# Layer 2's output product of an attention-and-two-layer kernel: which operand stands in the array, and the layout of the stored result

## The chip, the cores and the metric

The kernel runs on one core of a Trainium2 chip. A core has five engines with queues of their own: TensorE (PE in the profile, with its weight loads as PEld), VectorE (DVE), ScalarE (ACT), GpSimd (POOL) and SyncE (SP), which issues the DMAs here. The metric is the device time of one execution in microseconds (us); lower is better. A matmul on TensorE loads one operand into the array (the stationary one, LDWEIGHTS, here mostly 128 x 128) and streams the other through it (the moving one, MATMUL, here of up to 512 columns), and adds the product into a bank of PSUM.

## The reference, cut to what matters

An attention-like recurrence gives 3072 tokens of width 384, and two feed-forward layers follow, each with 2048 hidden units:

```python
def _moe_ref(x, w_in, w_out):          # layer 1: x is 3072 x 384
    h = x @ w_in                       # 384 x 2048
    g = h - np.tanh(h)
    return (g @ w_out).astype(np.float32)

def _moe2_ref(x, w_in, w_out):         # layer 2
    h = x @ w_in
    r = np.maximum(h, 0.0)
    g = r * r
    return (g @ w_out).astype(np.float32)   # 2048 x 384: the result is 3072 x 384
```

## The kernel before, in words

Each product is made of three matmuls. Every operand is split into a high part and a small remainder (`gh` and `gl` of the activations, `wh` and `wl` of the weights, `xh` and `xl` of the input), all in the 4-byte type fp32r, and high x high, high x low and low x high are added up in PSUM.

The tokens are worked on in six groups of 512 (`TG`), and the 2048 hidden units in sixteen slices of 128 (`NM`). One slice of one group is a **block**; there are 96 blocks of layer 1 (the very first in two halves) and then 96 of layer 2. A block has two products:

- `g1` (L197): the hidden slice `h`, 128 hidden units as rows by 512 tokens. Nine matmuls of 512 columns, weights stationary, input moving. Both layers do it in the same way.
- `g2` (L221 to L238): the slice's share of the group's result, added into banks `acc` that stay open over the sixteen blocks of a group. Layer 1 (L230 to L232) keeps the weights stationary and lets the 512 tokens of `gh` or `gl` move: nine matmuls of 512 columns into three banks, with the model's 128-column pieces as rows. Layer 2 (L236 to L238) does the reverse: 128 tokens of `gh` or `gl` are stationary and the weights' 384 model columns move: twelve matmuls of 384 columns into four banks, with the tokens as rows.

Between the two products `act` (L204) turns `h` into `gh` and `gl`: in layer 2 relu (L215), square (L216) and a copy to `gh` (L217) on ScalarE, then the remainder `gl` (L218) on VectorE.

`block_step(t)` (L850) writes the work down in a software pipeline: `act` of block t-1, `g1` of block t, and then `g2` of a block two or, from the last group of layer 1 on, three steps back. The engines run their queues in order. While layer 1 runs, TensorE does attention work between the blocks; in layer 1's last group and in all of layer 2 it does nothing but `g1` and `g2`, one after the other.

At the end of a group the banks are copied to SBUF and stored. Layer 1 does it in `put_x2` (L246): three banks of 512 columns, the first and third copied by ScalarE (L250), the second by VectorE (L252). Layer 2 does it in `put_out` (L272): four banks of 384 columns, two copied by ScalarE (L276) and two by VectorE (L278), each then stored by one DMA of SP's queue (L279) into 128 rows of the 3072 x 384 result. `new_acc` (L240) takes the banks: three of the pool `ps_c`, which has just three, and for layer 2 one more of `ps_a`. So the next group's first matmul into a bank must wait until the bank has been copied out.

In layer 2 ScalarE also makes one pass (`conv_check`, L174) over a reloaded weight block every second block; SP loads these blocks (L173), two buffers deep, in the same queue as the stores. `judge` (L911) folds the checks into a flag with one tiny matmul near the end. `run_general` (L646) is a slow path behind that flag, which is not taken.

Of the kernel before, what the change touches and what calls it, by code (L numbers as in the profile page):

```python
# [12 lines left out]
F32 = mybir.dt.float32  # L13
# [4 lines left out]
ALU = mybir.AluOpType  # L18
# [14 lines left out]
def kernel(  # L33
# [8 lines left out]
):  # L42
    nc = tc.nc
    B, S, H, DP = v.shape
    NT, DM = out.shape
    D = DM // H
    P = 128
    FF = w1.shape[0] * P
# [3 lines left out]
    KD = DM // P  # L52
    TG = B * P
# [12 lines left out]
    ps_c = fctx.enter_context(tc.tile_pool(name="ps_c", bufs=3, space=PSUM))  # L66
    ps_a = fctx.enter_context(tc.tile_pool(name="ps_a", bufs=3, space=PSUM))
# [9 lines left out]
        out=mask, in_=mask, compare_op=ALU.is_ge, fill=0.0, base=0,  # L77
# [55 lines left out]
    def words(st):  # L133
        sv = st.rearrange("p (n two) -> p n two", two=2)
        return sv[:, :, 0], sv[:, :, 1]
# [85 lines left out]
    def g2(layer, m, g, acc, cs=slice(0, TG)):  # L221
        gh, gl = g
        wh, wl = (w_[:, DM:] for w_ in wts[layer, m])
        first = m <= 0 and cs.start == 0
        end = m in (-1, NM - 1)
        if layer == 0:
            for j in range(KD):
                sl = slice(j * P, (j + 1) * P)
                o = acc[j][:, cs]
                nc.tensor.matmul(o, wh[:, sl], gh, start=first, stop=False)  # L230
                nc.tensor.matmul(o, wh[:, sl], gl, start=False, stop=False)  # L231
                nc.tensor.matmul(o, wl[:, sl], gh, start=False, stop=end)  # L232
        else:
            for j in range(B):
                sl = slice(j * P, (j + 1) * P)
                nc.tensor.matmul(acc[j][:, :DM], gh[:, sl], wh, start=first, stop=False)  # L236
                nc.tensor.matmul(acc[j][:, :DM], gh[:, sl], wl, start=False, stop=False)  # L237
                nc.tensor.matmul(acc[j][:, :DM], gl[:, sl], wh, start=False, stop=end)  # L238

    def new_acc(layer):  # L240
        acc = [ps_c.tile([P, TG], F32, tag="c", name="acc") for _ in range(KD)]
        if layer == 1:
            acc.append(ps_a.tile([P, TG], F32, tag="a", name="acc3"))
        return acc

    def put_x2(acc, dst):  # L246
        for j in range(KD):
# [12 lines left out]
    def split_x(xpool, xf):  # L260
        xh = xpool.tile([P, KD, TG], F32R, tag="xh", name="xh")
        xl = xpool.tile([P, KD, TG], F32R, tag="xl", name="xl")
        for kk in range(KD):
            nc.gpsimd.tensor_scalar(
                xh[:, kk], xf[:, kk], 1.0, 0.0, op0=ALU.mult, op1=ALU.add
            )
            nc.vector.tensor_tensor(
                xl[:, kk], xf[:, kk], xh[:, kk].bitcast(F32), op=ALU.subtract
            )
        return xh, xl  # L270

    def put_out(ap3, acc, dst):  # L272
        for j in range(B):
            t = ap3.tile([P, TG], F32, tag="ot", name="ot", bufs=4)
            if j % 2 == 0:
                nc.scalar.copy(t[:, :DM], acc[j][:, :DM])  # L276
            else:
                nc.vector.tensor_copy(t[:, :DM], acc[j][:, :DM])  # L278
            nc.sync.dma_start(dst(j), t[:, :DM])  # L279


    chk_s = const.tile([P, NU], F32, name="chk_s")
# [352 lines left out]
    for n in range(B, NU):  # L635
        c, b = divmod(n, B)
# [9 lines left out]
    def run_general():  # L646
# [5 lines left out]
        with ExitStack() as es:  # L652
            cp = es.enter_context(tc.tile_pool(name="gc", bufs=1))
# [8 lines left out]
            with tc.For_i(0, S, 1) as t:  # L662
# [15 lines left out]
                r = cp.tile([BH, D], F32, name="g_r")  # L678
# [18 lines left out]
                for i in range(NB):  # L697
                    sl = slice(i * TG, (i + 1) * TG)
# [16 lines left out]
                for i in range(NB):  # L715
                    sl = slice(i * TG, (i + 1) * TG)
# [7 lines left out]
        for layer in range(2):  # L724
            with ExitStack() as es:
                cp = es.enter_context(tc.tile_pool(name=f"gw{layer}", bufs=1))
                pp = es.enter_context(tc.tile_pool(name=f"gq{layer}", bufs=1, space=PSUM))
                na = KD + layer
                with tc.For_i(0, NG, 1) as g:
                    xf = cp.tile([P, KD, TG], F32, name="g_xf")  # L730
                    if layer == 0:
                        for j in range(B):
                            xn = cp.tile([P, DM], F32, name=f"g_xn{j}")
                            nc.sync.dma_start(xn, xg[ds(g * TG + j * P, P), :])
                            px = pp.tile([P, TG], F32, tag="h", name=f"g_px{j}")
                            for kk in range(KD):
                                sl = slice(kk * P, (kk + 1) * P)
                                nc.tensor.transpose(px[:, sl], xn[:, sl], ident)
                            nc.vector.tensor_copy(
                                xf[:, :, j * P:(j + 1) * P],  # L740
                                px[:, :DM].rearrange("p (k t) -> p k t", k=KD),
                            )
                    else:
                        nc.sync.dma_start(
                            xf, xg2.rearrange("k p t -> p k t")[:, :, ds(g * TG, TG)]
                        )
                    xt = split_x(cp, xf)
                    osum = cp.tile([P, na, TG], F32, name="g_os")
                    nc.vector.memset(osum, 0.0)
                    with tc.For_i(0, NM, 1) as m:  # L750
                        st = cp.tile([P, 2 * n2], I32, name="g_st")
                        nc.sync.dma_start(
                            st.unsqueeze(1),
                            (w1, w2)[layer].bitcast(I32).rearrange("m p x -> p m x")[:, ds(m, 1)],
                        )
                        lo, hi = words(st)
                        u = cp.tile([P, n2], I32, name="g_u")
                        uf = u.bitcast(F32)
                        ts, st2 = nc.vector.tensor_scalar, nc.vector.scalar_tensor_tensor
                        ts(u, hi, 0x7FFFFFFF, None, op0=ALU.bitwise_and)  # L760
                        ts(uf, uf, CLAMP_LO, CLAMP_HI, op0=ALU.max, op1=ALU.min)
                        ts(u, u, 3, 0x40000000, op0=ALU.logical_shift_left, op1=ALU.bitwise_xor)
                        st2(u, lo, 29, u, op0=ALU.logical_shift_right, op1=ALU.bitwise_or)
                        ts(u, u, 0x7FFFFFFF, None, op0=ALU.bitwise_and)
                        st2(u, hi, -0x80000000, u, op0=ALU.bitwise_and, op1=ALU.bitwise_or)
                        wh = cp.tile([P, n2], F32R, name="g_wh")
                        wl = cp.tile([P, n2], F32R, name="g_wl")
                        split_w(wh, wl, uf)
                        wts[layer, -1] = (wh, wl)
                        h = g1(layer, -1, xt, pp.tile([P, TG], F32, tag="h", name="g_h"))  # L770
                        acc = [
                            pp.tile([P, TG], F32, tag=f"c{j}", name=f"g_acc{j}")
                            for j in range(na)
                        ]
                        g2(layer, -1, act(layer, h, cp), acc)
                        for j, a in enumerate(acc):
                            n = TG if layer == 0 else DM
                            nc.vector.tensor_tensor(
                                osum[:, j, :n], osum[:, j, :n], a[:, :n], op=ALU.add
                            )  # L780
                    for j in range(na):
                        if layer == 0:
                            nc.sync.dma_start(xg2[j, :, ds(g * TG, TG)], osum[:, j])
                        else:
                            nc.sync.dma_start(
                                out[ds(g * TG + j * P, P), :], osum[:, j, :DM]
                            )


# [22 lines left out]
        return lambda j: x2g[g][j]  # L812

    def out_dst(g):
        return lambda j: out[j * S + g * P:j * S + (g + 1) * P, :]

    HT = TG // 2
    LAG = 3
# [11 lines left out]
    cur = {"g2": 0, "acc": None, "pool": gpool, "recheck": 0}  # L830
# [8 lines left out]
    def second_half(n):  # L839
        l, g, m, cs = blocks[n]  # L840
        if m == 0 and cs.start == 0:
            cur["acc"] = new_acc(l)
        g2(l, m, gs.pop(n), cur["acc"], cs)
        if m == NM - 1:
            if l == 0:
                put_x2(cur["acc"], x2_dst(g))
            else:
                put_out(cur["pool"], cur["acc"], out_dst(g))
# [94 lines left out]


_INS = ["qk", "v", "ri", "w1", "w2"]
_OUTS = [((3072, 384), "float32")]

# [45 lines left out]
```

## Time and profile before

| | |
|---|---|
| median of 3 runs | 1036.13 us (1034.98 to 1036.3) |
| the profiled execution's own time | 1037.15 us |
| its span, first to last instruction | 1035.1 us |
| TensorE busy in the span | 1004.8 us (97%) |
| ScalarE, VectorE busy | 641.4 us (62%), 565.5 us (55%) |
| mean granted TensorE clock | 0.998 of full speed |

The span is the time between the first and the last instruction that the profile records; the rest of an execution's own time lies around it. A matmul's duration in the profile runs from its start to the modelled end of its output, and matmuls overlap: what TensorE spends on one is the distance from its start to the next start, and that is read from the timeline.

### The profile page before, as it was taken

How to read it: one execution, taken by the hardware profiler on the slowest of the kernel's cores; microseconds unless marked ns; L12 is line 12 of the kernel's file. 1: busy time of each engine (PE TensorE's matmuls, PEld its weight loads, DVE VectorE, ACT ScalarE, POOL GpSimd, SP SyncE). 2: the span in 40 equal slices, each digit the busy share in tenths (PEclk: the TensorE clock that was granted, in tenths of full speed). 3: DMA queues.
4: the chain of work that ended last, by engine and by line, in shares of the span. 5: the costliest groups of instructions: out<-in, count | busy, mean ns of one | idle time of the engine just before them, and what ended most of it. 6: DMA issues, size and time to landing. Idle time of an engine off the chain costs nothing.

```text
span 1035.1 us, 16245 instructions
## 1 busy us (share of the span) xinstructions
PE 1004.8 (97%) x6388; PEld 863.0 (83%) x6388; DVE 565.5 (55%) x937; ACT 641.4 (62%) x1158; POOL 17.1 (2%) x35
## 2 busy tenths in 40 slices
PE   4998999999999999999999999999999999999997
PEld 1786777888888888888888888999999999999997
DVE  7989998877887665666544554122232322322211
ACT  8688887877776677677543446445555555555442
POOL 1000000000000000000000000000000000000000
PEclk9999999999999999999999999999999999999999
DMA  7324353544453211112004332013242242330000
GB/s 262 110 88 143 133 161 135 182 156 134 163 179 104 71 63 51 43 41 67 28 25 170 120 106 93 1 62 123 92 155 99 103 131 94 100 114 31 31 1 34
DMA packets 34642, 103.47 MB, mean 100 GB/s; under 512 B 5376, under 2 KB 8448, under 8 KB 34560
## 3 DMA queue, kind: packets, MB, share of 16 engines
q1 hardware_dynamic: 34560, 102.38, 29.3%
q8 instruction: 51, 0.84, 0.3%
q14 instruction: 31, 0.25, 0.1%
HBM read 86.51 MB, written 15.73 MB: 99 GB/s over the span
## 4 chain that ended last, share of the span: by engine, by line
PE 83%; DVE 2%; DMA 1%; ACT 1%; issue 0%; ACTq 0%
PE h L197 35%; PE acc L236 7%; PE acc L238 7%; PE acc L237 6%; PE acc L232 5%; PE acc L231 5%; PE acc L230 5%; PE px L566 3%; PE sc L533 3%; PE pU L597 2%; PE pq L516 1%; PE pk L516 1%; DMA ri<-in_ri_dram 1%; PE pc L427 0%; DVE cv L150 0%; DVE cv L146 0%
## 5 line engine op out<-in xcount | busy, mean ns | idle before, releaser
L218 DVE TENSOR_TENSOR gl<-t,gh 128x512 fp32r<-128x512 f32 (+1 forms) x193 | 132.5, 687 | 262.7 <-ACT gh L217 262.4
L197 PE MATMUL h<-xh,wh 128*128 128x512 f32 (+1 forms) x579 | 231.6, 400 | 0.1
L197 PE MATMUL h<-xh,wl 128*128 128x512 f32 (+1 forms) x579 | 227.7, 393 | 0.0
L197 PE MATMUL h<-xl,wh 128*128 128x512 f32 (+1 forms) x579 | 227.2, 392 | 0.0
L217 ACT CAST gh<-t 128x512 fp32r<-128x512 f32 (+1 forms) x193 | 119.3, 618 | 67.7 <-PE acc L237 43.3
L215 ACT ACTIVATE t<-h 128x512 f32<-128x512 f32 x96 | 57.5, 599 | 143.8 <-PE h L197 143.8
L238 PE MATMUL acc<-wh,gl 128*128 128x384 f32 x384 | 129.5, 337 | 0.0
L236 PE MATMUL acc<-wh,gh 128*128 128x384 f32 x384 | 129.4, 337 | 0.0
L237 PE MATMUL acc<-wl,gh 128*128 128x384 f32 x384 | 128.9, 336 | 0.0
L197 PEld LDWEIGHTS h<-xh,wl 128*128 128x128 f32 x579 | 108.7, 188 | 23.3
L197 PEld LDWEIGHTS h<-xh,wh 128*128 128x128 f32 x579 | 109.0, 188 | 21.9 <-issue 3.2
L197 PEld LDWEIGHTS h<-xl,wh 128*128 128x128 f32 x579 | 109.0, 188 | 18.1
L230 PE MATMUL acc<-gh,wh 128*128 128x512 f32 (+1 forms) x291 | 111.0, 391 | 3.1 <-ACT gh L217 3.1
L231 PE MATMUL acc<-gl,wh 128*128 128x512 f32 (+1 forms) x291 | 113.5, 390 | 0.3 <-DVE gl L218 0.3
L232 PE MATMUL acc<-gh,wl 128*128 128x512 f32 (+1 forms) x291 | 113.4, 390 | 0.0
L110 ACT ACTIVATE t<-h 128x512 f32<-128x512 f32 (+1 forms) x97 | 57.2, 590 | 79.1 <-PE h L197 77.5
L213 DVE TENSOR_TENSOR t<-h,t 128x512 f32<-128x512 f32 (+1 forms) x97 | 66.1, 682 | 42.2 <-ACT t L110 41.7
L103 ACT ACT_TABLE_LOAD x64 | 82.1, 1283 | 1.9 <-PEq L981 0.8
L236 PEld LDWEIGHTS acc<-wh,gh 128*128 128x128 f32 x384 | 72.2, 188 | 4.2
L237 PEld LDWEIGHTS acc<-wl,gh 128*128 128x128 f32 x384 | 72.1, 188 | 4.1
L238 PEld LDWEIGHTS acc<-wh,gl 128*128 128x128 f32 x384 | 72.0, 188 | 0.0
L230 PEld LDWEIGHTS acc<-gh,wh 128*128 128x128 f32 x291 | 54.2, 188 | 13.8 <-ACT gh L217 4.1
(133 smaller groups left out, 1406.3 us busy)
## 6 DMA issues: line engine op xcount, KB each, us to landing
st<-in_w_dram SPq DMA_DIRECT2D x32, 768.0 KB
sr<-in_w_dram SPq DMA_DIRECT2D x32, 768.0 KB
ri<-in_ri_dram SPq DMA_DIRECT2D x24, 384.0 KB
qk<-in_qk_dram SPq DMA_DIRECT2D x24, 384.0 KB
w2d<-cv SPq DMA_DIRECT2D x16, 384.0 KB
jw<-w2d SPq DMA_DIRECT2D x16, 384.0 KB
vz<-in_v_dram SPq DMA_DIRECT2D x21, 256.0 KB
x2d<-x2t SPq DMA_DIRECT2D x18, 256.0 KB
```

Source lines behind the costliest of these rows:

```text
L103: load = nc.scalar.preload_act_table_set(name).ins
L197: nc.tensor.matmul(h, w_[:, kk * P:(kk + 1) * P], x_[:, kk, cs], start=(i == 0), stop=(i == n - 1),)
L213: nc.vector.tensor_tensor(t, h, t, op=ALU.subtract)
L215: last["act"] = nc.scalar.activation(t, h, AF.Relu).ins
L217: nc.scalar.copy(gh, t)
L218: nc.vector.tensor_tensor(gl, t, gh.bitcast(F32), op=ALU.subtract)
L230: nc.tensor.matmul(o, wh[:, sl], gh, start=first, stop=False)
L231: nc.tensor.matmul(o, wh[:, sl], gl, start=False, stop=False)
L232: nc.tensor.matmul(o, wl[:, sl], gh, start=False, stop=end)
L236: nc.tensor.matmul(acc[j][:, :DM], gh[:, sl], wh, start=first, stop=False)
L237: nc.tensor.matmul(acc[j][:, :DM], gh[:, sl], wl, start=False, stop=False)
L238: nc.tensor.matmul(acc[j][:, :DM], gl[:, sl], wh, start=False, stop=end)
```

## The change

Layer 2's `g2` is written as layer 1's is: the weights are stationary, the 512 tokens of `gh` and `gl` move, and each block has nine matmuls of 512 columns into three banks. The result then stands with the model's columns as rows, so the output tensor becomes 384 x 3072 and is stored by three DMAs a group; a tile's 512 tokens belong to four batches of 128, which lie apart in the result, so each of a tile's 128 rows goes out as four pieces of 128 numbers. The caller turns the array over on the host, outside the measured time. The slow path behind the flag is changed in the same way and is left out of the diff.

```diff
@@ kernel
-    NT, DM = out.shape
+    DM, NT = out.shape
@@ g2
-        if layer == 0:
-            for j in range(KD):
-                sl = slice(j * P, (j + 1) * P)
-                o = acc[j][:, cs]
-                nc.tensor.matmul(o, wh[:, sl], gh, start=first, stop=False)
-                nc.tensor.matmul(o, wh[:, sl], gl, start=False, stop=False)
-                nc.tensor.matmul(o, wl[:, sl], gh, start=False, stop=end)
-        else:
-            for j in range(B):
-                sl = slice(j * P, (j + 1) * P)
-                nc.tensor.matmul(acc[j][:, :DM], gh[:, sl], wh, start=first, stop=False)
-                nc.tensor.matmul(acc[j][:, :DM], gh[:, sl], wl, start=False, stop=False)
-                nc.tensor.matmul(acc[j][:, :DM], gl[:, sl], wh, start=False, stop=end)
-
-    def new_acc(layer):
-        acc = [ps_c.tile([P, TG], F32, tag="c", name="acc") for _ in range(KD)]
-        if layer == 1:
-            acc.append(ps_a.tile([P, TG], F32, tag="a", name="acc3"))
-        return acc
+        for j in range(KD):
+            sl = slice(j * P, (j + 1) * P)
+            o = acc[j][:, cs]
+            nc.tensor.matmul(o, wh[:, sl], gh, start=first, stop=False)
+            nc.tensor.matmul(o, wh[:, sl], gl, start=False, stop=False)
+            nc.tensor.matmul(o, wl[:, sl], gh, start=False, stop=end)
+
+    def new_acc():
+        return [ps_c.tile([P, TG], F32, tag="c", name="acc") for _ in range(KD)]
@@ put_out
-        for j in range(B):
+        for j in range(KD):
             t = ap3.tile([P, TG], F32, tag="ot", name="ot", bufs=4)
             if j % 2 == 0:
-                nc.scalar.copy(t[:, :DM], acc[j][:, :DM])
+                nc.scalar.copy(t, acc[j])
             else:
-                nc.vector.tensor_copy(t[:, :DM], acc[j][:, :DM])
-            nc.sync.dma_start(dst(j), t[:, :DM])
+                nc.vector.tensor_copy(t, acc[j])
+            nc.sync.dma_start(dst(j), t.rearrange("p (b t) -> p b t", b=B))
@@ out_dst
-        return lambda j: out[j * S + g * P:j * S + (g + 1) * P, :]
+        return lambda j: out[j * P:(j + 1) * P, :].rearrange("p (b s) -> p b s", b=B)[
+            :, :, g * P:(g + 1) * P
+        ]
@@ second_half
-            cur["acc"] = new_acc(l)
+            cur["acc"] = new_acc()
@@ the caller
-    return r.results[0]["out_0_dram"]
+    return _np.ascontiguousarray(r.results[0]["out_0_dram"].T)
```

Up to layer 2's first `g2` every engine's order stays as it was. Line numbers of the changed kernel are its own: its `g2` is L229 to L231 and its copies L266 and L268, its store L269. On TensorE, `g2` of the fourth block of a group in layer 2; a row is line, operation, bank<-moving,stationary, and the moving operand's rows x columns. Before:

```order
L236 MATMUL acc_6920<-wh1_3_5981,gh_6942 128x384
L237 MATMUL acc_6920<-wl1_3_5982,gh_6942 128x384
L238 MATMUL acc_6920<-wh1_3_5981,gl_6943 128x384
L236 MATMUL acc_6921<-wh1_3_5981,gh_6942 128x384
L237 MATMUL acc_6921<-wl1_3_5982,gh_6942 128x384
L238 MATMUL acc_6921<-wh1_3_5981,gl_6943 128x384
L236 MATMUL acc_6922<-wh1_3_5981,gh_6942 128x384
L237 MATMUL acc_6922<-wl1_3_5982,gh_6942 128x384
L238 MATMUL acc_6922<-wh1_3_5981,gl_6943 128x384
L236 MATMUL acc3_6923<-wh1_3_5981,gh_6942 128x384
L237 MATMUL acc3_6923<-wl1_3_5982,gh_6942 128x384
L238 MATMUL acc3_6923<-wh1_3_5981,gl_6943 128x384
```

The same block after:

```order
L229 MATMUL acc_6868<-gh_6886,wh1_3_5981 128x512
L230 MATMUL acc_6868<-gl_6887,wh1_3_5981 128x512
L231 MATMUL acc_6868<-gh_6886,wl1_3_5982 128x512
L229 MATMUL acc_6869<-gh_6886,wh1_3_5981 128x512
L230 MATMUL acc_6869<-gl_6887,wh1_3_5981 128x512
L231 MATMUL acc_6869<-gh_6886,wl1_3_5982 128x512
L229 MATMUL acc_6870<-gh_6886,wh1_3_5981 128x512
L230 MATMUL acc_6870<-gl_6887,wh1_3_5981 128x512
L231 MATMUL acc_6870<-gh_6886,wl1_3_5982 128x512
```

The operands have changed places, the fourth bank `acc3` is gone, and `gl` is wanted by the second matmul instead of the third. On ScalarE, the block in which the first group's banks of layer 2 are copied out, with relu, the check's pass, copies, square and cast; before:

```order
L215 ACTIVATE t_6903<-h_6869 128x512
L174 ACTIVATE cz0_1_6937,chk_v_125<-sr0_1_6936 128x768
L276 COPY ot_6891<-acc_6425 128x384
L276 COPY ot_6897<-acc_6427 128x384
L216 ACTIVATE t_6903<-t_6903 128x512
L217 CAST gh_6904<-t_6903 128x512
```

The same place after:

```order
L215 ACTIVATE t_6851<-h_6823 128x512
L174 ACTIVATE cz0_1_6881,chk_v_125<-sr0_1_6880 128x768
L266 COPY ot_6842<-acc_6425 128x512
L216 ACTIVATE t_6851<-t_6851 128x512
L266 COPY ot_6848<-acc_6427 128x512
L217 CAST gh_6852<-t_6851 128x512
```

The copies are of whole banks, and the second now stands behind the square. On SP, the first group's stores of layer 2 among the loads of the check; before:

```order
L173 DMA sr_2_6999<-in_w_dram 128x1536
L173 DMA sr_3_7062<-in_w_dram 128x1536
L279 DMA out_dram<-ot 128x384 x4
L173 DMA sr_4_7125<-in_w_dram 128x1536
L173 DMA sr_5_7188<-in_w_dram 128x1536
```

The same place after:

```order
L173 DMA sr_2_6937<-in_w_dram 128x1536
L173 DMA sr_3_6994<-in_w_dram 128x1536
L269 DMA out_dram<-ot 512x1x128 x3
L173 DMA sr_4_7051<-in_w_dram 128x1536
L173 DMA sr_5_7108<-in_w_dram 128x1536
```

Three stores of 512 pieces of 128 numbers (512 bytes) stand where four of 128 pieces of 384 numbers (1536 bytes) stood; their place among the loads is the same.

## Rows read from the trace of the kernel before

**Rows 1.** The page: span, engines (busy us, share, instructions), chain of waits by engine.

```profile
span 1035.1 us, 16245 instructions
PE 1004.8 (97%) x6388; PEld 863.0 (83%) x6388; DVE 565.5 (55%) x937; ACT 641.4 (62%) x1158; POOL 17.1 (2%) x35
PE 83%; DVE 2%; DMA 1%; ACT 1%; issue 0%; ACTq 0%
```

**Rows 2.** Windows: layer 1's last group, layer 2; busy us (instructions), PEclk, DMA share, GB/s.

```profile
562.00:603.00 41.00, 41.00 (x183) 33.95 (x182) 24.50 (x33) 19.02 (x31) 2.22 (x3) 1.00 0.43 150
640.00:1020.00 380.00, 380.00 (x1907) 344.36 (x1907) 97.76 (x149) 196.85 (x347) 8.88 (x12) 1.00 0.23 77
```

**Rows 3.** Timeline of TensorE, one block of layer 1's last group (start, duration, what).

```profile
570.02 0.39 PE L230 MATMUL acc<-gh,wh 128*128 128x512 f32 x1
...
572.06 0.39 PE L197 MATMUL h<-xh,wh 128*128 128x512 f32 x1
...
574.10 0.39 PE L230 MATMUL acc<-gh,wh 128*128 128x512 f32 x1
```

**Rows 4.** Timeline of TensorE, one block of layer 2.

```profile
702.29 0.33 PE L236 MATMUL acc<-wh,gh 128*128 128x384 f32 x1
...
704.39 0.39 PE L197 MATMUL h<-xh,wh 128*128 128x512 f32 x1
...
706.48 0.33 PE L236 MATMUL acc<-wh,gh 128*128 128x384 f32 x1
```

**Rows 5.** Timeline of TensorE and VectorE: layer 2's first and last blocks of the product.

```profile
635.30 0.33 PE L236 MATMUL acc<-wh,gh 128*128 128x384 f32 x1
...
1020.47 0.33 PE L236 MATMUL acc<-wh,gh 128*128 128x384 f32 x1
...
1022.06 0.33 PE L236 MATMUL acc<-wh,gh 128*128 128x384 f32 x1
...
1024.14 0.33 PE L236 MATMUL acc<-wh,gh 128*128 128x384 f32 x1
...
1028.97 0.34 PE L238 MATMUL acc<-wh,gl 128*128 128x384 f32 x1
1029.35 0.56 DVE L278 COPY ot<-acc 128x384 f32<-128x384 f32 x1 [0.49 <-PE acc L238]
```

**Rows 6.** Timeline of three engines where layer 2's first group ends.

```profile
698.10 0.33 PE L236 MATMUL acc<-wh,gh 128*128 128x384 f32 x1
...
698.80 0.89 ACT L174 ACTIVATE cz<-sr 128x768 bf16<-128x768 f32 x1
...
699.37 0.56 DVE L278 COPY ot<-acc 128x384 f32<-128x384 f32 x1 [1.92 <-PE acc L238]
...
699.68 0.84 ACT L276 COPY ot<-acc 128x384 f32<-128x384 f32 x2
...
700.42 0.64 ACT L216 ACTIVATE t<-t 128x512 f32<-128x512 f32 x1
```

**Rows 7.** Layer 1's copies by line: ns min/median/max, first and last start.

```profile
L250 ACT COPY x2t<-acc x12: 571/588/593, 179.4 to 634.0; 128x512 f32<-128x512 f32 x12
L252 DVE COPY x2t<-acc x6: 676/692/692, 179.7 to 632.8; 128x512 f32<-128x512 f32 x6
```

**Rows 8.** Waits of TensorE, then of SP: us in total, times, longest us.

```profile
PE acc L230 <- ACT gh L217: 3.1, 2, 2.3
SPq L173 <- ACT cz L174: 209.4, 29, 8.0
```

**Rows 9.** DMA queue in 1028:1034 and 690:698: packets, MB, share of 16 engines; then L279's issues.

```profile
q1 hardware_dynamic: 576, 0.79, 37.0%
q1 hardware_dynamic: 544, 1.57, 53.5%
L279 SPq DMA_DIRECT2D out_dram<-ot x24: 332/418/948, 700.2 to 1029.9; - x24
```

More of the change, by code (lines that the diff above doesn't have):

```diff
@@ L727, in run_general @@
                 pp = es.enter_context(tc.tile_pool(name=f"gq{layer}", bufs=1, space=PSUM))
-                na = KD + layer
                 with tc.For_i(0, NG, 1) as g:
@@ L747, in run_general @@
                     xt = split_x(cp, xf)
-                    osum = cp.tile([P, na, TG], F32, name="g_os")
+                    osum = cp.tile([P, KD, TG], F32, name="g_os")
                     nc.vector.memset(osum, 0.0)
@@ L772, in run_general @@
                             pp.tile([P, TG], F32, tag=f"c{j}", name=f"g_acc{j}")
-                            for j in range(na)
+                            for j in range(KD)
                         ]
@@ L776, in run_general @@
                         for j, a in enumerate(acc):
-                            n = TG if layer == 0 else DM
                             nc.vector.tensor_tensor(
-                                osum[:, j, :n], osum[:, j, :n], a[:, :n], op=ALU.add
+                                osum[:, j], osum[:, j], a, op=ALU.add
                             )
-                    for j in range(na):
+                    for j in range(KD):
                         if layer == 0:
@@ L785, in run_general @@
                             nc.sync.dma_start(
-                                out[ds(g * TG + j * P, P), :], osum[:, j, :DM]
+                                out[j * P:(j + 1) * P, ds(g * TG, TG)], osum[:, j]
                             )
@@ L945 @@
 _INS = ["qk", "v", "ri", "w1", "w2"]
-_OUTS = [((3072, 384), "float32")]
+_OUTS = [((384, 3072), "float32")]
 def _arrange(q, k, v, a_re, a_im, moe_w_in, moe_w_out, moe2_w_in, moe2_w_out):
```

## The prediction

> **What bounds the kernel now.** The page comes first: TensorE is busy for 97% of the span, and the chain of work that ended last is TensorE for 83% of it; no other engine has more than 2% [rows 1]. The windows show the stage that the change touches: between 640 and 1020 us, which is nearly all of layer 2, TensorE is busy for the whole 380 us at the full granted clock (1.00, the 2.4 GHz level), while ScalarE works for 197 us and VectorE for 98 us [rows 2]. So layer 2 lasts as long as its matmuls take to start one after the other, and only a change of their pace can move the end. Busy time and duration don't tell that pace, because matmuls overlap (a matmul of 512 columns is shown with 0.39 us and the next one starts long before that is over); the starts in the timeline do. Three of them tell most of it. In layer 1's last group, where TensorE also does nothing but the two products, all in matmuls of 512 columns, the block from one first L230 to the next takes 574.10 - 570.02 = 4.08 us; nine matmuls take 2.04 us, in either product, 0.227 us each [rows 3]. In layer 2 a block takes 706.48 - 702.29 = 4.19 us: 2.10 us for the twelve of 384 columns, and 2.09 us for the nine of 512 columns, which are the same instructions that took 2.04 us in layer 1 [rows 4]. And where twelve of 384 columns follow others of 384, behind the last `g1`, they take 1024.14 - 1022.06 = 2.08 us, 0.173 us each [rows 5].
>
> Two things can be read from that. First, the columns are equal (9 x 512 = 12 x 384 = 4608), but a matmul has a part that doesn't go with its columns: (0.227 - 0.173) / 128 columns is 0.42 ns a column, and 0.227 us less 512 of these leaves some 11 to 13 ns for each matmul; three matmuls fewer save 0.04 us a block (2.08 against 2.04). Second, in the mixed stream both products are slower than each is by itself: 4.19 instead of 2.08 + 2.04 = 4.12 us. Some 0.07 us a block goes where the width changes, twice in a block, and most of that falls on `g1`, which the change doesn't edit.
>
> **The change, part by part.** The matmuls first. After the change layer 2's stream has the form of layer 1's last group: eighteen matmuls of 512 columns, weights stationary, tokens moving, out of the same tiles. I take its block at 4.08 us. The mean block of layer 2 before, from the first product to the last one with a `g1` behind it, is (1020.47 - 635.30) / 92 = 4.187 us [rows 5]. So 92 blocks save 0.107 us each, 9.8 us, and the four products that have no `g1` behind them save 0.04 us each, 0.2 us. Together **10.0 us**. All of it lies on the path, since TensorE waits for nothing in this stage [rows 2]; that goes on being so if `gh`, `gl` and the banks come in time.
>
> `gl` is wanted one matmul earlier, 0.2 us. The product runs three blocks, some 12 us, behind its `g1`, and relu, square, cast and remainder of one block are over within the next one or two, so this is hidden; if that cover were gone, the price would be at most these 0.2 us a block. ScalarE and VectorE are asked for the same activations in 4.08 us instead of 4.19; by the windows ScalarE is then at 53% instead of 52%.
>
> The banks at a group's end: before, three of the four came out of `ps_c`, as now, so the rule that the next group waits for the copies is not new. Now to the times. Take the first group's end [rows 6]: the last product starts at 698.10, and at the new pace its banks are full at about 698.9, 699.6 and 700.3 (the third, sixth and ninth start, and 0.39 us). ScalarE is held by the check's pass up to 699.68, as before; then come the first copy, 0.59 us by layer 1's row [rows 7], the square (0.64 us), and the second copy, which ends at about 701.5; VectorE's copy (0.69 us) ends at about 700.3. The next group's first product starts 2.04 us behind the end of this one, at 702.2, and wants its banks at 702.2, 702.9 and 703.5. So the slack is 1.9, 2.6 and 2.0 us, and nothing waits. Layer 1 has just this form, three banks and the same three copies, and the longest waits of TensorE on `acc` are on `gh` (L230, two times, 3.1 us in all), none on a copy [rows 8]. I cost the copies at nothing, at five borders; what is queued behind the later second copy on ScalarE is the cast of a block that is used three blocks later.
>
> SP issues three stores instead of four among the check's loads. An issue took 0.33 to 0.95 us [rows 9]; four times the pieces could make that longer, and behind the stores stands the next load for the check, for which ScalarE would have to wait in order. But that load is issued far ahead: SP itself waits for ScalarE to give a buffer back, 29 times and up to 8 us [rows 8]. I cost it at nothing.
>
> The last store is on the path. Its copy is now ScalarE's (0.59 against 0.56 us), and the last matmul is longer by 0.06 us: 0.1 us. Then the store: 512 pieces of 512 bytes instead of 128 of 1536, so 32 pieces on each of the 16 DMA engines instead of 8. No row shows a store in such small pieces. From the two rows of the queue [rows 9]: 37.0% of 16 engines over 6 us is 35.5 us for 576 packets of 0.79 MB, 62 ns each at 1.37 KB; 53.5% over 8 us is 68.5 us for 544 packets of 1.57 MB, 126 ns each at 2.9 KB. The line through the two is 3.4 ns and 42.5 ns a KB, which gives 25 ns for a piece of 512 bytes. By bytes alone it would be 22 ns; the upper bound is a whole packet's 62 ns. The three stores are issued three matmuls apart, 0.68 us, and take 32 x 25 = 0.8 us each, so the last one ends 3 x 0.8 - 1.36 = 1.0 us behind its issue instead of 0.5. With 0.1 us of copy that is **0.6 us** more at the end (0.3 by the low bound, 6.0 - 1.4 - 0.5 + 0.1 = 4.2 by the high one). I take the line, since two packet sizes with a factor of two between them lie so near to it. The end behind that (flag, barriers) stays.
>
> **Sum.** 1037.15 - 10.0 + 0.6 = 1027.7 us against the profiled execution's own time, whose span is 1035.1. The median of the runs lies 1.0 us under that execution, so against 1036.13 the forecast is **1026.8 us** (-0.9%).
>
> **The rivals.** *The pace of layer 2 isn't due to the mixed widths.* The nine `g1` matmuls are slower in layer 2 by 0.005 us each, and this could come from something else there (the activations' traffic, the check's loads). Then eighteen would take 2 x 2.09 = 4.18 us, 92 blocks would save 0.007 us each and the last ones 0.2, 0.8 us in all, of which the end takes 0.6: 1035.9 us, no change. For it: the edit doesn't touch these instructions. Against it: layer 1's last group has more DMA (0.43 against 0.23) and more of VectorE's work in the same time [rows 2] and keeps 0.227 us.
>
> *Only columns count.* Then the equal columns would give the same block and the end's 0.6 us would be all: 1036.7 us. The rows of pure streams, 0.227 and 0.173 us, speak against it. The Trainium skill (TensorE: Matmul & The Clock Gate, section Back-to-back issue gap) says that warm matmuls follow each other at N / 2.4 GHz and about 2.5 ns; by that rule nine of 512 and twelve of 384 columns differ by 8 ns, an estimate of 0.7 us for 96 blocks, and the kernel would end at about 1036 us; the trace doesn't agree, with 11 to 13 ns where the page has 2.5.
>
> *The stores pile up at the end.* This is the slower case. If a piece of 512 bytes takes p, the end grows by 96 p - 1.36 - 0.5 + 0.1 us. It eats the whole gain at p = 122 ns and makes the kernel measurably slower from 144 ns on; with 150 ns the time is 1036.1 - 10.0 + 12.6 = 1038.7 us. For it: the pieces go to rows that lie 12 KB apart, and no store of before is scattered so. Against it: the packets of 2.9 KB take only 126 ns.
>
> That the change doesn't do what it says is excluded by the order of instructions, in which nine stand for twelve in every block of layer 2.
>
> **How the numbers follow.** The forecast, with the end anywhere in its bounds, 0.84; layer 2's pace stays 0.08; columns only 0.04; stores pile up 0.04. A measurement of this kernel can tell some 0.2% (2.1 us) from no change. The first is faster in all of its range (1036.1 - 10.0 + 4.2 = 1030.3 at most); the two of the pace are within 0.2%; the last is slower. So faster 0.84, same 0.12, slower 0.04. The range goes down to 0.3 us for the end and the lowest of the runs shown, 1.2 us under their median (1025.3), a little further for a mean block of 4.07, and up to 1030.3 and a little for the spread of runs: 1024.8 to 1031.0. It leaves the rivals out, 0.16.
>
> **What the changed profile would show.** Starts of all matmuls of layer 2 0.227 us apart, in both products, and 4.08 us a block without exception, is the forecast; `g1` at 0.232 would be the first rival. From the first product of layer 2 at 635.3 to the last matmul's start there should be 1028.97 - 635.30 - 10.0 = some 383.7 us. TensorE's waits should have no row from a copy of `ot` to `acc`; one would be the border price that I took as nothing. From the last matmul's start to the span's end there were 1035.1 - 1028.97 = 6.1 us; I expect 6.7, and over 8 would say that the pieces cost a packet's time. What would make it wrong as a whole: a granted clock under 1.00 in layer 2 now that its stream is denser.

## The result, and the profile after

| | before | after |
|---|---|---|
| median (lowest to highest of 6 runs) | 1036.07 us (1034.98 to 1038.11) | 1027.11 us (1026.16 to 1029.02) |
| ratio to the kernel before, 95% interval | | 0.9914 (0.9901 to 0.9927) |
| the profiled execution's own time | 1037.15 us | 1027.04 us |
| its span | 1035.1 us | 1025.0 us |
| first product of layer 2 to the last matmul's start | 393.67 us | 383.66 us |
| the last matmul's start to the span's end | 6.1 us | 7.2 us |

To the hundredth the spans are 1035.11 and 1025.05 us; the last row goes by these.

The forecast was 1026.8 us, the range 1024.8 to 1031.0. The page of the changed kernel, as [rows 1] of before: span, engines, and the chain by engine. TensorE has 288 matmuls fewer and is the bound as it was.

```profile
span 1025.0 us, 15616 instructions
PE 993.2 (97%) x6100; PEld 821.8 (80%) x6100; DVE 563.2 (55%) x931; ACT 641.9 (63%) x1158; POOL 17.1 (2%) x35
PE 84%; DVE 2%; DMA 0%; ACT 0%; issue 0%
```

The windows of layer 1's last group and of layer 2, as [rows 2]: the granted clock stays at 1.00 in the denser stream, and TensorE is busy all the time.

```profile
562.00:603.00 41.00, 41.00 (x183) 33.95 (x182) 24.86 (x34) 19.75 (x31) 1.55 (x2) 1.00 0.41 139
630.00:1010.00 380.00, 380.00 (x1678) 314.65 (x1677) 99.19 (x149) 202.66 (x357) 8.89 (x12) 1.00 0.24 79
```

The timeline of TensorE where layer 2's product begins, as [rows 3 to 5]. Product, `g1`, product:

```profile
634.20 0.39 PE L229 MATMUL acc<-gh,wh 128*128 128x512 f32 x1
634.42 0.39 PE L230 MATMUL acc<-gl,wh 128*128 128x512 f32 x1
634.65 0.39 PE L231 MATMUL acc<-gh,wl 128*128 128x512 f32 x1
...
636.24 0.39 PE L197 MATMUL h<-xh,wh 128*128 128x512 f32 x1
636.47 0.39 PE L197 MATMUL h<-xl,wh 128*128 128x512 f32 x1
...
638.28 0.39 PE L229 MATMUL acc<-gh,wh 128*128 128x512 f32 x1
...
1009.56 0.39 PE L229 MATMUL acc<-gh,wh 128*128 128x512 f32 x1
...
1017.86 0.39 PE L231 MATMUL acc<-gh,wl 128*128 128x512 f32 x1
```

638.28 - 634.20 = 4.08 us a block, 2.04 us for each of the two products: `g1`, which the change doesn't edit, is as fast as in layer 1. From 634.20 to 1009.56 there are 92 blocks, (1009.56 - 634.20) / 92 = 4.080 us each, where [rows 5] gave 4.187. Nothing varies over them, at the groups' ends neither.

So 10.0 us went out of layer 2, and 1.1 us came back behind the last matmul. The remaining 1.1 us between the two spans lies ahead of the change: this execution's first product of layer 2 starts at 634.20 instead of 635.30. That start differs from execution to execution of kernels whose work up to there is the same (by 3 us over the profiles of this study) and isn't the change's.

### The profile page after: what moved, and what is told of

The parts are those of the page before. It is cut to its first block, busy times and chain, and to the rows that moved or that the text cites. A ratio compares the mean times of both kernels' runs of the same rounds, so it can differ in the third digit from the quotient of the medians.

```text
span 1025.0 us, 15616 instructions
## 1 busy us (share of the span) xinstructions
PE 993.2 (97%) x6100; PEld 821.8 (80%) x6100; DVE 563.2 (55%) x931; ACT 641.9 (63%) x1158; POOL 17.1 (2%) x35
## 4 chain that ended last, share of the span: by engine, by line
PE 84%; DVE 2%; DMA 0%; ACT 0%; issue 0%
PE h L197 36%; PE acc L229 12%; PE acc L231 12%; PE acc L230 12%; PE px L556 4%; PE sc L523 3%; PE pU L587 2%; PE pq L506 1%; PE pk L506 1%; DMA ri<-in_ri_dram 0%; PE pc L417 0%; PE pu L417 0%; PE pu L418 0%; PE pc L418 0%; PE pU L583 0%; DVE cv L150 0%
## 5 line engine op out<-in xcount | busy, mean ns | idle before, releaser
L229 PE MATMUL acc<-gh,wh 128*128 128x512 f32 (+1 forms) x579 | 223.2, 390 | 3.3 <-ACT gh L217 3.3
L230 PE MATMUL acc<-gl,wh 128*128 128x512 f32 (+1 forms) x579 | 225.6, 390 | 0.3 <-DVE gl L218 0.3
L231 PE MATMUL acc<-gh,wl 128*128 128x512 f32 (+1 forms) x579 | 225.4, 389 | 0.0
L229 PEld LDWEIGHTS acc<-gh,wh 128*128 128x128 f32 x579 | 108.3, 188 | 25.3 <-ACT gh L217 4.4
L231 PEld LDWEIGHTS acc<-gh,wl 128*128 128x128 f32 x579 | 108.7, 188 | 22.6 <-issue 0.2
L230 PEld LDWEIGHTS acc<-gl,wh 128*128 128x128 f32 x579 | 108.7, 188 | 22.2 <-DVE gl L218 1.2
L216 ACT ACTIVATE t<-t 128x512 f32<-128x512 f32 x96 | 60.4, 630 | 2.0
L177 DVE TENSOR_TENSOR wmin<-wmin,cz 128x768 bf16<-128x768 bf16 x32 | 17.8, 557 | 57.4 <-ACT cz L174 57.4
L523 PEld LDWEIGHTS sc<-qT,kT 128*128 128x128 f32 x352 | 42.4, 191 | 2.0 <-ACT kT L513 0.5
L523 PE MATMUL sc<-qT,kT 128*128 128x128 f32 x352 | 43.3, 276 | 0.0
```

Of the source, the lines that this page charges most:

```text
L216: nc.scalar.activation(t, t, AF.Square)
L523: nc.tensor.matmul(sc[:, j, :], T("kT", i)[:, j, :], T("qT", i)[:, j, :], start=True, stop=True)
```

## The experiments

**The theory** is that of the prediction: a matmul costs its columns and a fixed part of some 13 ns, and a change of width between matmuls slows the next ones, on both sides of the change. **The rival** is that something else in layer 2 slowed its matmuls: tokens as the stationary operand, or the other engines' traffic. The first run changes nothing but the number of width changes, the second nothing but the width, the third the number of matmuls.

**Half as many changes of width.** The kernel before, layer 2's blocks in pairs:

```diff
-        while cur["g2"] < NB and cur["g2"] <= t - (LAG if t >= NATT + 2 else 2):
+        lag = LAG if t >= NATT + 2 else 2
+        if t >= NATT + NM + LAG:
+            lag = 2 if t % 2 == 0 else NB
+        while cur["g2"] < NB and cur["g2"] <= t - lag:
```

> The kernel before, with layer 2's blocks taken in pairs: two g1, then two products of twelve 384-column matmuls. Every matmul, operand and bank is as before; only the number of places where the width changes is halved. If a change of width is what costs (some 0.067 us for the two changes of a block), a pair takes 2 x 4.187 - 0.067 = 8.307 us and 46 pairs save 3.1 us: 1033.0 us against 1036.1, with nine g1 matmuls still slow behind each change and the second nine of a pair at 0.227 us. If layer 2's matmuls are slower for another reason (traffic, tokens as the stationary operand), a pair takes 8.37 us and nothing is saved: 1036 us.

Measured: 1032.71 us, ratio 0.996 (0.9947 to 0.9974) to the kernel before. Its timeline of TensorE, one pair:

```profile
703.57 0.33 PE L236 MATMUL acc<-wh,gh 128*128 128x384 f32 x1
...
705.67 0.33 PE L236 MATMUL acc<-wh,gh 128*128 128x384 f32 x1
...
707.75 0.39 PE L197 MATMUL h<-xh,wh 128*128 128x512 f32 x1
...
709.83 0.39 PE L197 MATMUL h<-xh,wh 128*128 128x512 f32 x1
...
711.87 0.33 PE L236 MATMUL acc<-wh,gh 128*128 128x384 f32 x1
```

The pair takes 711.87 - 703.57 = 8.30 us where two blocks of before take 8.37. The first product behind a change takes 2.10 us, the second 2.08; the first `g1` 2.08, the second 2.04. By the trace 46 pairs save 3.1 us; by the medians it is 4.0 us, with an interval of 2.7 to 5.5. The same instructions with the same operands are faster when no change of width stands ahead of them. That is the theory's number, and the rival, by which nothing would move, falls.

**Wide instead of narrow.** The kernel before, the twelve matmuls at 512 columns; 128 columns of each are computed for nothing and not copied out:

```diff
+        w5h, w5l = (w_[:, n2 - TG:] for w_ in wts[layer, m])
...
-                nc.tensor.matmul(acc[j][:, :DM], gh[:, sl], wh, start=first, stop=False)
-                nc.tensor.matmul(acc[j][:, :DM], gh[:, sl], wl, start=False, stop=False)
-                nc.tensor.matmul(acc[j][:, :DM], gl[:, sl], wh, start=False, stop=end)
+                nc.tensor.matmul(acc[j], gh[:, sl], w5h, start=first, stop=False)
+                nc.tensor.matmul(acc[j], gh[:, sl], w5l, start=False, stop=False)
+                nc.tensor.matmul(acc[j], gl[:, sl], w5h, start=False, stop=end)
...
```

> The kernel before, with the twelve matmuls of layer 2's product widened from 384 to 512 columns (128 columns of the other weight piece go along, into a part of the bank that is not copied out). Tokens stay stationary, there are still twelve matmuls and four banks; only the width is now that of g1. If the change of width costs, all 21 matmuls of a block start 0.227 us apart, 4.76 us a block, g1 included, and the time is 1036 + 92 x 0.573 + 2.6 = 1091 us. If tokens as stationary operand or layer 2's other work cost, g1 stays at 0.232 us or the product is slower than 0.227 us: 4.87 us a block, 1101 us.

Measured, one run: 1092.03 us. Its timeline of TensorE:

```profile
701.75 0.39 PE L237 MATMUL acc<-wh,gh 128*128 128x512 f32 x1
...
704.47 0.39 PE L197 MATMUL h<-xh,wh 128*128 128x512 f32 x1
...
706.51 0.39 PE L237 MATMUL acc<-wh,gh 128*128 128x512 f32 x1
```

706.51 - 701.75 = 4.76 us a block; `g1` takes 2.04 us, and the twelve 2.72, which is 0.227 each. Tokens are stationary, layer 2's other work is there, and no matmul is slow. So it is not the exchange of the operands that gains: what it brings is that the moving side has 512 columns.

**More and narrower.** The changed kernel, each matmul of layer 2's product cut in two (the slow path keeps the old form):

```diff
...
+                for i in range(2):
+                    hf = slice(i * TG // 2, (i + 1) * TG // 2)
+                    o = acc[j][:, hf]
+                    nc.tensor.matmul(o, wh[:, sl], gh[:, hf], start=first and i == 0, stop=False)
+                    nc.tensor.matmul(o, wh[:, sl], gl[:, hf], start=False, stop=False)
+                    nc.tensor.matmul(o, wl[:, sl], gh[:, hf], start=False, stop=end and i == 1)
...
```

> The changed kernel, with each of the nine 512-column matmuls of layer 2's product cut into two of 256. Columns and operands are the same, the number of matmuls and weight loads is doubled. If a matmul costs 0.417 ns a column and a fixed part of some 13 ns, one of 256 takes 0.120 us, the product 2.16 instead of 2.04 us, and with the changes of width a block takes some 4.27 us: 1027 + 18 = 1045 us. If only columns count, 4.08 us and 1027 us. If the weight load, 0.188 us in the profile, is what a short matmul waits for, the product takes 18 x 0.188 = 3.4 us, a block 5.4 us, and the time is some 1155 us.

Measured, one run: 1043.34 us. Its timeline of TensorE:

```profile
700.14 0.28 PE L232 MATMUL acc<-gh,wh 128*128 128x256 f32 x1
700.25 0.28 PE L233 MATMUL acc<-gl,wh 128*128 128x256 f32 x1
...
701.09 0.28 PE L234 MATMUL acc<-gh,wl 128*128 128x256 f32 x1
701.21 0.28 PE L232 MATMUL acc<-gh,wh 128*128 128x256 f32 x1
...
702.29 0.40 PE L197 MATMUL h<-xh,wh 128*128 128x512 f32 x1
...
704.36 0.28 PE L232 MATMUL acc<-gh,wh 128*128 128x256 f32 x1
```

A matmul of 256 columns takes 0.120 us (701.21 - 701.09), and so lies on one line with 0.173 for 384 and 0.227 for 512: 0.42 ns a column and 13 ns. The product takes 2.15 us, 0.11 more than nine of 512, which is nine times the fixed part. The third theory, that the weight load (shown with 0.19 us in this run too) sets the pace of short matmuls, falls at this width. The block takes 704.36 - 700.14 = 4.22 us, 0.05 less than I expected: behind 256 columns `g1` takes 2.07 us, not 2.09, and the product loses nothing behind 512 columns.

**Pieces of the store.** The changed kernel, with the stores in rows of 2,048 bytes; the caller then reorders the tokens on the host, and the slow path, which isn't taken, is not adapted:

```diff
-            nc.sync.dma_start(dst(j), t.rearrange("p (b t) -> p b t", b=B))
+            nc.sync.dma_start(dst(j), t)
...
-        return lambda j: out[j * P:(j + 1) * P, :].rearrange("p (b s) -> p b s", b=B)[
-            :, :, g * P:(g + 1) * P
-        ]
+        return lambda j: out[j * P:(j + 1) * P, g * TG:(g + 1) * TG]
...
```

> The changed kernel, with each bank's 512 columns stored as 128 pieces of 2,048 bytes instead of 512 of 512 bytes (the tokens of a group then lie side by side in the result, and the caller puts them in their order on the host, outside the measured time). From the last matmul's start to the span's end the changed kernel took 7.1 us. If the number of pieces costs, here through the later first packet (1.2 us behind the issue instead of 0.84) and through longer transfers (32 x 28 ns on an engine instead of 8 x 84 ns), it takes 6.2 to 6.4 us, and the time is 1026.3 us. If the longer copy and the longer matmuls made the end later, it stays at 7.1.

**Last banks one by one.** The changed kernel, with the last two products taken bank by bank:

```diff
...
+    def last_two():
+        p, q = gs.pop(NB - 2), gs.pop(NB - 1)
+        for j in range(KD):
+            g2(1, NM - 2, p, cur["acc"], js=(j,))
+            g2(1, NM - 1, q, cur["acc"], js=(j,))
+            put_out(cur["pool"], cur["acc"], out_dst(NG - 1), js=(j,))
...
```

> The changed kernel, with the last two products of the last group taken bank by bank, so that the three last banks are full six matmuls (1.36 us) apart instead of three (0.68 us). The stores keep their 512-byte pieces. If the stores wait for each other at the end (0.89 us of transfer each, issued 0.68 us apart), the last matmul's start lies 0.4 to 0.5 us nearer to the span's end: 6.7 us instead of 7.1. If it is the time from an issue to its first packet alone, nothing moves.

Measured, one run each: 1026.11 and 1028.26 us, which tell nothing of a difference this small; the ends of the traces do. The changed kernel's end, SP and ScalarE in the timeline (the last matmul's start stands above, 1017.86):

```profile
1017.54 2.02 SPq L269 DMA_DIRECT2D out_dram<-ot  x3
...
1018.28 0.58 ACT L266 COPY ot<-acc 128x512 f32<-128x512 f32 x1 [0.77 <-PE acc L231]
```

Its DMA traffic in 40 slices of 0.2 us from 1016 on (GB/s), and the queue (packets, MB, share of 16 engines):

```profile
GB/s 0 0 0 0 0 0 0 0 0 0 0 0 0 44 297 274 282 297 284 307 261 292 279 295 279 297 287 200 41 38 3 41 0 0 0 0 0 0 41 0
...
q1 hardware_dynamic: 1584, 0.79, 35.7%
```

With pieces of 2,048 bytes, the page's span, the timeline, and the traffic in the same slices:

```profile
span 1024.1 us, 15616 instructions
```

```profile
1017.34 1.69 SPq L269 DMA_DIRECT2D out_dram<-ot  x3
...
1017.66 0.39 PE L231 MATMUL acc<-gh,wl 128*128 128x512 f32 x1
```

```profile
GB/s 0 0 0 0 0 0 0 0 0 0 51 328 399 369 226 307 348 440 338 389 348 277 51 102 31 20 31 0 0 0 0 41 0 41 0 0 0 0 0 0
...
q1 hardware_dynamic: 432, 0.79, 27.0%
```

And bank by bank, in the same three views:

```profile
span 1026.3 us, 15616 instructions
```

```profile
1019.48 0.39 PE L231 MATMUL acc<-gh,wl 128*128 128x512 f32 x1
```

```profile
GB/s 0 0 0 0 0 0 0 82 41 0 0 0 0 0 15 261 294 289 289 162 0 0 148 282 317 279 241 69 95 279 287 300 277 156 15 0 0 41 0 0
```

From the last matmul's start to the span's end (spans to the hundredth): 7.2 us for the changed kernel (7.1 in the expectations, which go by the page's 1025.0), 1024.12 - 1017.66 = 6.5 with the long pieces, 1026.28 - 1019.48 = 6.8 bank by bank. So the pieces are worth 0.7 us and the bank order 0.4, from one trace each; the next run below, which leaves the end as the changed kernel has it, took 7.2 us there again. In the changed kernel the stores are one block of traffic at some 285 GB/s, so they do queue up; bank by bank there are gaps between the three. The pieces themselves cost 35.7% of 16 engines over 8 us in 1584 packets, 29 ns each. And the first bytes come some 1.2 us behind the first issue (1017.54, bytes from 1018.7 on), with the long pieces some 0.8 us (1017.34, 1018.1). The copies have no part in the 0.7 us, since the long pieces keep them.

How this reaches the span's end is not what the two expectations have in mind. Behind its last store SP branches past the slow path (the `if` on the flag, L930) and then asks for the DMAs' semaphores, one instruction each. These rows in the changed kernel, then in the kernel before:

```profile
L930 SPq EVENT_SEMAPHORE  x8: 17/17/17, 1023.1 to 1023.7; - x8
...
L930 SPq COMPARE_BRANCH  x1: 45/45/45, 1019.6 to 1019.6; - x1
```

```profile
L940 SPq EVENT_SEMAPHORE  x8: 17/17/17, 1033.2 to 1033.7; - x8
...
L940 SPq COMPARE_BRANCH  x1: 45/45/45, 1030.3 to 1030.3; - x1
```

The eight follow each other without a stop, and all stores have landed before the first of them: by the trace's semaphore records 0.6 us before it in the changed kernel, 0.9 in the kernel before, 0.3 with the long pieces. So the end doesn't wait for the last store to land. Behind the last matmul's start the branch comes after 1.75 us (before: 1.34, long pieces: 1.42), SP's next instruction 3.51 us later (2.86, 3.10), and the end 1.9 us after that in all three. The later branch follows the issue of the last store, which takes 0.65 us with 512 pieces and 0.33 with 128. What SP waits for behind the branch isn't shown; in each of the nine traces a packet of the DMA queue `instruction` ends 1.1 to 1.3 us before SP goes on, so it is likely that it waits for its next instructions and that these come later among the stores' packets. No run tests that.

**Fewer changes of shape in layer 1.** In layer 1 attention's narrow matmuls stand between those of 512 columns, which is the same thing in another place. The changed kernel, with one stage of attention moved behind another:

```diff
-            (16, "p", a13), (16, "v", a13v),
+            (15, "p", a13), (15, "v", a13v),
```

> The changed kernel, with one stage of layer 1's attention work (the state update of a unit, L583 and L587 and its VectorE part) moved one block earlier, directly behind the output product of the same unit (L556). No work is added or left out; 16 times two short stretches of narrow matmuls between the 512-column ones become one. If a change of shape on TensorE costs as the trace shows it around these stretches (0.09 us in front, 0.09 us behind, and a little in the matmuls after), 16 fewer save some 2.4 to 3.2 us against the changed kernel: 1024.3 us, a ratio to the kernel before of 0.989. If it costs nothing or the update now comes too early for its inputs, 1027 us or more.

Measured: 1026.02 us, ratio 0.9894 (0.9879 to 0.991), against 0.9914 for the changed kernel; the intervals overlap. The stretch in which it acts can be read off by itself in TensorE's timeline, from the first `g1` of layer 1's second group to the first of layer 2. The changed kernel, then this one:

```profile
169.64 0.63 PE L197 MATMUL h<-xh,wh 128*128 128x512 f32 x2
...
619.92 0.39 PE L197 MATMUL h<-xh,wh 128*128 128x512 f32 x1
```

```profile
169.91 0.63 PE L197 MATMUL h<-xh,wh 128*128 128x512 f32 x2
...
619.17 0.39 PE L197 MATMUL h<-xh,wh 128*128 128x512 f32 x1
```

450.28 and 449.26 us: 1.0 us saved. By the widths in the traces, eleven of the sixteen stretches of narrow matmuls that went in the whole kernel lie here, so that is 0.09 us for each, where I expected 0.15 to 0.2. TensorE's waits in this stretch of the new kernel (us in total, times, longest us); the changed kernel has none there:

```profile
PE pk L506 <- DVE kn L495: 1.0, 2, 0.8
PE pq L506 <- DVE qn L495: 0.5, 2, 0.3
```

So `pk` and `pq` now wait four times, 1.5 us in all. If these waits took the gain one for one, the stretch would be 2.5 us shorter without them; that isn't shown.

**All three edits together** (the stage, the long pieces, the last banks):

> The changed kernel with three edits: the state update of layer 1's attention directly behind its output product (which took 1.1 us off the median by itself), pieces of 2,048 bytes in the stores, and the last two products bank by bank. If the savings add up, 1.1 and some 0.8 to 0.9 us at the end: 1025.2 us, a ratio of 0.9885 to the kernel before. With 2,048-byte pieces the stores take 0.67 us each and don't queue up at 0.68 us apart, so the bank-by-bank order should add nothing to the pieces.

Measured: 1024.78 us, ratio 0.989 (0.9873 to 0.9906). It is the fastest median of the study, and faster than the kernel before; against the changed kernel's 0.9914 (0.9901 to 0.9927) its interval overlaps, so that it beats that one too is likely and not shown by the times. In the trace its end takes 6.2 us (1024.24 - 1018.00), 0.2 less than with the long pieces alone, where I expected nothing from the bank order.

## Why the prediction was right

- **The pace of layer 2, right to the hundredth.** 4.08 us a block was taken from layer 1's rows, and 4.080 came; 383.7 us from the first product to the last matmul, and 383.66 came. The way in which the gain was split (0.04 us a block for three matmuls fewer, 0.07 for the changes of width) is confirmed in both parts: the pairs take back half of the second part, and the cut matmuls pay the first.
- **The first rival** (layer 2's own traffic) fell with the pairs and with the wide matmuls.
- **The second** (columns only) fell with the matmuls of 256 columns: the fixed part is 13 ns in three widths. The trace goes on disagreeing with the Trainium skill (TensorE: Matmul & The Clock Gate, section Back-to-back issue gap), where the formula for the gap of isolated matmuls has a fixed part of about 2.5 ns; by that formula the change would have been worth under 1 us, an estimate.
- **The banks at the groups' ends, right.** In the changed kernel's timeline of the first group's end, the second copy of ScalarE ends at 698.54, and the third bank is wanted six matmuls behind the next product's start, at 699.48 + 1.36 = 700.8: 2.3 us of slack where I had 2.0.

```profile
697.96 0.58 ACT L266 COPY ot<-acc 128x512 f32<-128x512 f32 x1
...
699.48 0.39 PE L229 MATMUL acc<-gh,wh 128*128 128x512 f32 x1
```

- **`gl`, ScalarE's load, SP's queue, right:** TensorE has no wait in layer 2.
- **The end was mis-sized, and its path was another.** The forecast had 0.6 us, 1.1 us came. The piece was sized well (25 ns against 29), and the stores do queue up (0.5 us in the sum; the bank order wins 0.4 back). But the sum let the last store's landing end the path and what stands behind it stay. In the traces the stores have landed before SP goes on, and what grew is SP's own way: its branch comes 0.41 us later, 0.32 of it the longer issue of the last store, and its next instruction another 0.65 us later behind the branch. The issues' row [rows 9] showed only how long an issue took, not how that grows with the pieces, and I costed it at nothing, having in mind the loads behind it in the queue and not the store itself.
- **The third rival** (stores that pile up) had a queue that is there and a price far too high; 29 ns a piece is a quarter of what it needed to eat the gain.

The sum came out 0.3 us under the measured median, with an end 0.5 us too small. That it lies as near as this is partly luck: the changed kernel's runs lie up to 2.9 us apart.

## What to carry to other kernels

Where TensorE is the bound, read the starts of its matmuls and not their durations, and look for the same instruction at two paces: here a product that nobody meant to touch was 2% slow because of the width of what stood next to it. Prefer the form that moves the most columns in each matmul and keeps the width the same along the stream; which operand stands in the array is then a question of layout. A transposed result costs at the store, in pieces; only the kernel's last stores cost time here, by the number of their pieces, and by the traces not through their landing but on the engine that issues them: a longer issue (0.65 us against 0.33 for the last one) and a longer wait behind its branch. So look at what the issuing engine still has to do after its last store.

## What the runs showed of the hardware that I had not expected

A change of width is paid over several matmuls behind it, not at once, and not in the order of the widths: a `g1` behind products of 384 columns takes 2.08 us (eight of its nine matmuls take 228 to 236 ns in the mean of layer 2, the fourth 224), behind 256 columns 2.07 (the first five take 229 to 236 ns), and behind its like 2.04 us (227 ns each). With 384 columns the change costs on both ways (2.10 instead of 2.08 us for the product), with 256 columns the product's first matmul starts its successor earlier (0.11 us instead of 0.120). What in TensorE makes this isn't shown by these runs. And a weight load that the profile shows with 0.19 us didn't hold up matmuls that follow each other every 0.120 us.
